# A first load in two parts, x by eight rows, and a piece of w_o cut once more, in a decode kernel of attention and a gated MLP

## The chip, the cores and the metric

The kernel runs on one core of one Trainium2 chip. The metric is the device time of one execution in microseconds. The profile comes from one execution taken by the hardware profiler; its times count from the start of the span. PE is TensorE's matmul, PEld its weight load, DVE VectorE, ACT ScalarE, POOL GpSimd, and SP SyncE, which issues most DMA transfers. One core has 16 DMA engines that all transfers share.

## What is computed

One decode step for two sequences (B = 2) of width D = 512. The normalised x feeds two branches, a windowed attention over a cache and a gated MLP; all data are float32. Cut to what matters:

```python
xn = layernorm(x)                                   # x: (2, 1, 512)
q  = xn @ wq                                        # wq: (512, 4096), 32 heads of 128
k, v = the last 4096 positions of k_cache, v_cache  # (2, 8, 4096, 128), each head used by 4 of q
s  = softmax(q @ k.T * 128 ** -0.5) @ v @ wo        # wo: (4096, 512)
z  = gelu(xn @ w_in)                                # w_in: (512, 1792)
h  = z[:896] * (w_sp * layernorm(z[896:]) + b_sp)   # w_sp and b_sp are single numbers
g  = silu(h @ w_out)                                # w_out: (896, 512)
out = x + s * g
```

The weights and the two windows together are 89.4 MB; all else is small.

## The kernel before

**Memory.** One tile `ring` (line 80) holds four slots of 32 KB in each of the 128 partitions. All large loads go through it in a fixed order: w_q in slots 0 and 1, w_in in 2, w_out in 3, then by turns the eight units of k and of v, then w_o. `enqueue` and `advance` (lines 85 to 99) issue a load on SP's queue as soon as its slots are free; a slot comes free where the code calls `advance` behind the last reader. SP issues in program order and waits at each load for the readers of the slot. Each load also waits, where eight transfers have been issued since, for the transfer that last used the same completion semaphore.

**Start.** w_q is one load of 128 rows, one row of 64 KB in each partition (`load_rows`, line 110). ScalarE issues the load of x as two rows of 512 (`xs`, lines 170 to 172), behind a tiny activation that makes its function table load early. VectorE takes mean and variance of x (`st`, `mv`, lines 210 to 213), `rsqrt` gives the scale `rs`, and a copy of it into the first element of slot 2 (line 219) makes the load of w_in wait until then. VectorE normalises (`xn`, line 233), PE turns it in four transposes into a PSUM tile, and a copy puts the two columns of each into the cleared `xnT` (lines 234 to 237), which has 32 columns per piece. The product with w_q (lines 268 to 276) needs `xnT` and all of w_q.

**Middle.** For each unit of k, VectorE turns the four quarters (`turn`), PE multiplies with q (`shares`, `add_shares`), ScalarE takes the exponentials (`probs`), and PE weighs v (`values`). The gated MLP runs ahead of the units. Small masks made on GpSimd (`same_r`, `sel`, `sel4`, `negm`) are used with the maxima of the units.

**End.** w_o is 32 blocks of rows, loaded in pieces (`load_blocks`, lines 147 to 163): one of sixteen blocks, one of eight, and a last slot with a piece of four and four single blocks. Behind the piece of sixteen SP also loads x again, as four rows for each sequence, into `x4`, which the last addition uses. The products with the first 28 blocks go to one PSUM tile `part` (lines 541 to 544), which is copied by ScalarE (`parts`) and spread by PE; the last four blocks go straight to `so`. Then come the multiplication with the gate, the addition of `x4`, and the store of the output from eight partitions (lines 557 to 560).

Lines in the profile: a helper records every operation of PE, DVE, ACT and SP, so all of these stand at line 37, and operations are told apart by their tiles.

Of the kernel before, what the change touches and what calls it, by code (L numbers as in the profile page):

```python
# [9 lines left out]
F32 = mybir.dt.float32  # L10
AF = mybir.ActivationFunctionType
ALU = mybir.AluOpType
AX = mybir.AxisListType

P = 128
HQ, DH = 32, 128
G = 4
# [4 lines left out]
def ap(t, offset, dims):  # L22

    return bass.AP(tensor=t.tensor, offset=t.offset + offset, ap=[list(t.ap[0])] + [list(d) for d in dims])
# [18 lines left out]
def kernel(  # L43
# [13 lines left out]
    nc = tc.nc  # L57
    pe, dve, act, sp = (InOrder(tc, e) for e in (nc.tensor, nc.vector, nc.scalar, nc.sync))
    B, _, D = x.shape
    _, HKV, SK, _ = k_cache.shape  # L60
    W = min(4096, max(256, SK // 4))
    REP = HQ // HKV
    F = w_in.shape[1]
    FH = F // 2
    KT = D // P
    FT = FH // P
    DC = D // G
# [5 lines left out]
    SLOT = J * DH  # L73
    BANKS = {"s": 2, "sh": 2, "acc": 2, "mo": 1, "col": 1}

    cst = ctx.enter_context(tc.tile_pool(name="cst", bufs=1))
# [3 lines left out]
    ring = cst.tile([P, 4 * SLOT], F32, tag="ring", name="ring")  # L80
# [4 lines left out]
    def enqueue(load, count=1):  # L85

        at = turns[0] % 4
        turns[0] += count
        queue.append((load, range(at, at + count)))
        advance()  # L90

    def advance(*slots):
        for n in slots:
            free[n] = True
        while queue and all(free[n] for n in queue[0][1]):
            load, at = queue.pop(0)
            for n in at:
                free[n] = False
            load(ring[:, at[0] * SLOT : (at[-1] + 1) * SLOT], at[0])

    def const(name, *shape):
        return cst.tile([P, *shape], F32, tag=name, name=name)

    def bank(name, tag):
        return ps.tile([P, 512], F32, tag=tag, name=name, bufs=BANKS[tag])
# [1 line left out]

    weight = {}

    def load_rows(name, w, k):  # L110
        def load(t, at):
            n = k * w.shape[1]
            sp.dma_start(t[:, :n], w.rearrange("(p k) f -> p (k f)", p=P))
            weight[name] = t[:, :n].rearrange("p (k f) -> p k f", k=k)

        return load

    enqueue(load_rows("q", wq, KT), 2)
    wqt = weight["q"]

    def by_group(t):
# [26 lines left out]
    blocks = []  # L148

    def load_blocks(piece):  # L150
        def load(t, at):
            t = t.rearrange("p (j d) -> p j d", d=D)
            a = 0
            for n in piece:
                j = len(blocks)
                sp.dma_start(t[:, a : a + n, :], wo_v[:, j : j + n, :])
                blocks.extend((t, a + i) for i in range(n))
                a += n
            if len(blocks) == 16:
                for b in range(B):  # L160
                    sp.dma_start(x4[16 * b : P : 32, :], x[b].rearrange("o (g c) -> (o g) c", g=G))

        return load


    ident = const("ident", P)
    make_identity(nc, ident)


    xs = cst.tile([B, D], F32, tag="xs", name="xs")  # L170
    act.activation(xs[:, 0:1], ident[:B, 0:1], AF.Ln, bias=1.0)
    act.dma_start(xs, x[:, 0, :])
    wb1 = cst.tile([1, 2], F32, tag="wb1", name="wb1")
    act.dma_start(wb1[:, 0:1], bass.AP(tensor=w_sp.tensor, offset=w_sp.offset, ap=[[1, 1], [1, 1]]))
    act.dma_start(wb1[:, 1:2], bass.AP(tensor=b_sp.tensor, offset=b_sp.offset, ap=[[1, 1], [1, 1]]))
    xnT = const("xnT", KT, 32)
    nc.gpsimd.memset(xnT, 0.0)
    ones = const("ones", P)
    nc.gpsimd.memset(ones, 1.0)
    hT = const("hT", FT, 32)  # L180
    nc.gpsimd.memset(hT, 0.0)
    x4 = const("x4", DC)
    nc.gpsimd.memset(x4, 0.0)
    add_dq = const("add_dq", NCH - 1 + P)
    nc.gpsimd.memset(add_dq, 0.0)
    sel = const("sel", 56)
# [10 lines left out]
    grpm = const("grpm", G)  # L197
    dve.tensor_reduce(grpm, ident.rearrange("p (g c) -> p g c", g=G), axis=AX.X, op=ALU.add)

    def rsqrt(dst, a, tag):  # L200
        t = cst.tile(list(a.shape), F32, tag="rt" + tag, name="rt" + tag)
        act.activation(t, a, AF.Ln)
        act.activation(dst, t, AF.Exp, scale=-0.5)
        dve.tensor_mul(t, dst, dst)
        dve.tensor_mul(t, t, a)
        dve.tensor_scalar(t, t, -0.5, 1.5, op0=ALU.mult, op1=ALU.add)
        dve.tensor_mul(dst, dst, t)


    st = cst.tile([B, nc.vector.BN_STATS_DIM], F32, tag="st", name="st")  # L210
    dve.bn_stats(st, xs)
    mv = cst.tile([B, nc.vector.BN_AGGR_DIM], F32, tag="mv", name="mv")
    dve.bn_aggr(mv, st)
    va = cst.tile([B, 1], F32, tag="va", name="va")
    dve.tensor_scalar_add(va, mv[:, 1:2], EPS)
    rs = cst.tile([B, 1], F32, tag="rs", name="rs")
    rsqrt(rs, va, "x")

    dve.tensor_copy(ring[:B, 2 * SLOT : 2 * SLOT + 1], rs)
    enqueue(load_rows("in", w_in, KT))  # L220
    enqueue(load_rows("out", w_out, FT))
    win, wout = weight["in"], weight["out"]
    for n in range(NU + 1):
# [2 lines left out]
        if n > 0:  # L226
            enqueue(load_unit(v_cache, units[n - 1], "v"))

    for piece in ((16,), (8,), (4, 1, 1, 1, 1)):
        enqueue(load_blocks(piece))  # L230

    xn = cst.tile([B, D], F32, tag="xn", name="xn")
    dve.tensor_scalar(xn, xs, mv[:, 0:1], rs, op0=ALU.subtract, op1=ALU.mult)
    pt = bank("xnT_ps", "sh")[:, : KT * B].rearrange("p (k b) -> p k b", k=KT)
    for k in range(KT):
        pe.transpose(pt[:, k, :], xn.rearrange("b (p k) -> b k p", k=KT)[:, k, :], ident[:B, :B])
    dve.tensor_copy(xnT[:, :, :B], pt)

    same = const("same", G, 32)
    nc.gpsimd.tensor_copy(same, ap(rowm, 0, [[0, G], [1, 32]]))  # L240
# [28 lines left out]
    for k in range(KT):  # L269
        for r in range(2):  # L270
            for g in range(G):
                c = (r * G + g) * 512
# [5 lines left out]
    qT = sb.tile([P, 1024], F32, tag="qT", name="qT", bufs=1)  # L278
# [3 lines left out]
    for gs in range(G):  # L282
        for b in range(B):
            dve.tensor_scalar_mul(
                ap(qm, b * 128 + gs // 2 * 32 + gs % 2 * 4, [[64, 2], [8, 4], [1, REP]]),
                ap(qT, b, [[512, 2], [32, 4], [128, REP]]), grpm[:, gs : gs + 1],
            )
    rp = bank("rp", "mo")[:, : 2 * B * 64]
    pe.matmul(rp, same, qm, start=True, stop=True)
# [23 lines left out]
    zt = const("zt", 2 * FT, 32)  # L313
    dve.transpose(zt.rearrange("p j c -> p (j c)"), ap(zs, 0, [[FQ, 2], [1, FT], [FT, 32]]))
    zT = const("zT", 2, FT, B)
    zTf = zT.rearrange("p h j b -> p (h j) b")
    dve.tensor_copy(zTf, zt[:, :, :B])
    uu = const("u", 2, FT, B)
    dve.tensor_mul(uu, zT, zT)
    dve.tensor_scalar(uu, uu, 0.044715, 1.0, op0=ALU.mult, op1=ALU.add)  # L320
# [34 lines left out]
    for j in range(FT):  # L355
        g = j % G
# [111 lines left out]
    def gather(b):  # L468

        hq = sb.tile([P, 32], F32, tag="hq", name=f"hq{b}")  # L470
        by_d = col[0][32 * b : 32 * b + 32, :].rearrange("p (j d) -> p d j", j=NCH)
        for e in range(4):
            dve.reduce_sum(hq[32 * e : 32 * e + 32, :], by_d[:, 32 * e : 32 * e + 32, :], axis=AX.X)
        t = bank(f"oT{b}", "acc")[:, :32]
        pe.matmul(t, perm, hq, start=True, stop=True)
        return t
# [56 lines left out]
    t = gather(last.b)  # L533
# [7 lines left out]
    for n in range(EARLY):  # L541
        t, a = blocks[n]
        g = n % G
# [4 lines left out]
    for n in range(EARLY, 32):  # L548
        if n == LATE:
            spread_quarters(so, parts, start=False, stop=False)  # L550
        t, a = blocks[n]
# [37 lines left out]
```

## Time and profile before

| | us |
|---|---|
| median of 3 runs | 218.07 (217.55 to 218.26) |
| span of the profiled execution | 215.6 |
| PE busy | 144.9 |
| DVE busy | 107.1 |
| ACT busy | 43.7 |
| POOL busy | 4.2 |
| share of the 16 DMA engines | 96.9% on the queue of SP |

The page gives for the profiled execution its span, 215.6 us; the device time of the runs holds some 2.5 us around such a span. A row of the chain of waits has a start, a length and what ran; a row of the timeline has a start, a length, the engine, the operation and its tiles, with the idle time before it and what ended that in brackets. A row of stretches has its bounds and its length, the busy time of five engines, the granted clock of PE, the mean busy share of the DMA engines and their GB/s; a packet's whole time counts in the stretch in which it starts, so a short stretch can show a share above 1. The queue table has packets, megabytes and the share of 16 engines' time; q1 is SP's queue, q10 that of ScalarE, q8 carries the fetches of instructions. Where a window is asked for, it starts with a row of GB/s in 40 equal slices of that window.

### The profile page before, as it was taken

The numbers are of one execution on the slowest core, as the hardware profiler recorded it, in microseconds if no ns is written. First come the engines' busy times: TensorE is split into PE (matmuls) and PEld (weight loads), VectorE is DVE, ScalarE is ACT, GpSimd is POOL, SyncE is SP. The second block draws the span as 40 slices with busy tenths as digits, with TensorE's granted clock in tenths as the row PEclk, the third lists the DMA queues.
The fourth block names the chain that finished last, engine by engine and source line by source line (L and its number), as shares of the span: only waits on it lengthen the run. The fifth ranks groups of instructions, "written<-read, shape, count | busy, mean of one in ns | idle before, by whom it ended". The sixth has DMA issues, their size and how long they took to land.

```text
span 215.6 us, 2181 instructions
## 1 busy us (share of the span) xinstructions
PE 144.9 (67%) x848; PEld 40.3 (19%) x848; DVE 107.1 (50%) x161; ACT 43.7 (20%) x108; POOL 4.2 (2%) x22
## 2 busy tenths in 40 slices
PE   0010787224595897699599499459949967987663
PEld 0010222100021222122122132112202211222311
DVE  1140025633995943953936663793585089233101
ACT  2030000331124115114303304130331231241001
POOL 6010000000000000000000000000000000000000
PEclk9999999658599699699799789859975996999998
DMA  9898999999999999999999999999999999999990
GB/s 389 390 389 389 431 423 459 435 438 421 450 395 474 395 453 419 444 432 425 439 404 450 419 444 429 432 432 419 444 413 447 425 432 444 425 435 404 410 376 33
DMA packets 3788, 89.52 MB, mean 415 GB/s; under 512 B 434, under 2 KB 450, under 8 KB 964
## 3 DMA queue, kind: packets, MB, share of 16 engines
q1 hardware_dynamic: 3772, 89.40, 96.9%
q8 instruction: 6, 0.10, 0.2%
q14 instruction: 2, 0.02, 0.0%
q10 hardware_dynamic: 8, 0.00, 0.0%
HBM read 89.40 MB, written 0.00 MB: 415 GB/s over the span
## 4 chain that ended last, share of the span: by engine, by line
DMA 41%; PE 39%; DVE 16%; ACT 2%; issue 2%; DVEq 0%
DMA ring<-in_A_wo_dram 20%; PE sh L37 11%; DMA ring<-in_A_k_cache_dram 11%; DVE kt L37 10%; DMA ring<-in_A_wq_dram 10%; PE s L37 10%; PE acc L37 7%; PE q_ps L37 4%; PE y L37 2%; PE z L37 1%; PE col L37 1%; PE mo L37 1%; DVE gate L37 1%; DVE u L37 1%; DVE qm L37 1%
## 5 line engine op out<-in xcount | busy, mean ns | idle before, releaser
L37 DVE STREAM_TRANSPOSE kt<-ring 128x2048 f32<-128x2048 f32 x32 | 72.2, 2286 | 24.9 <-DMA ring<-in_A_k_cache_dram 24.9
L37 PE MATMUL sh<-kt,qbd 128*32 128x512 f32 x256 | 43.6, 725 | 27.0 <-DVE kt L37 27.0
L37 ACT ACTIVATE shs<-sh 128x512 f32<-128x512 f32 x32 | 19.1, 597 | 99.4 <-PE sh L37 99.4
L37 PE MATMUL s<-shs,add_dq 128*128 128x512 f32 x64 | 39.0, 716 | 0.0
L37 PE MATMUL acc<-ring,pT 128*32 128x512 f32 x256 | 31.3, 614 | 0.0
L37 PEld LDWEIGHTS s<-shs,add_dq 128*128 128x128 f32 x64 | 11.0, 215 | 30.9 <-issue 26.5
L37 PEld LDWEIGHTS sh<-kt,qbd 128*32 128x32 f32 x256 | 7.0, 117 | 46.3 <-issue 38.3
L37 PE MATMUL q_ps<-ring,xnT 128*32 128x512 f32 x64 | 8.8, 713 | 7.6 <-DMA ring<-in_A_wq_dram 7.6
L37 PEld LDWEIGHTS acc<-ring,pT 128*32 128x32 f32 x256 | 7.8, 112 | 22.3 <-issue 17.6
L37 DVE TENSOR_REDUCE m<-s 128x2 f32<-128x512 f32 x8 | 5.4, 680 | 13.0 <-PE s L37 12.9
L37 PE MATMUL xnT_ps<-ident,xn 2*128 2x2 f32 x4 | 0.6, 252 | 14.5 <-DVE xn L37 14.5
L37 ACT ACTIVATE o<-acc,diag 128x128 f32<-128x128 f32 x30 | 8.6, 374 | 4.9 <-PE acc L37 4.9
L37 PE MATMUL part<-ring,oT 128*32 128x512 f32 x56 | 6.6, 597 | 3.5 <-DMA ring<-in_A_wo_dram 3.5
L37 ACT ACTIVATE p<-s,nb 128x256 f32<-128x256 f32 x16 | 7.6, 488 | 6.6 <-DVE nb L37 6.4
L37 DVE STREAM_TRANSPOSE qT<-q_ps 128x512 f32<-128x512 f32 x2 | 1.4, 717 | 14.4 <-PE q_ps L37 14.3
L37 PE MATMUL col<-o,sel 128*32 128x512 f32 x14 | 7.3, 601 | 0.0
L37 DVE TENSOR_TENSOR res<-so,gate 128x128 f32<-128x128 f32 x1 | 0.3, 292 | 11.5 <-PE so L37 11.5
L37 DVE STREAM_TRANSPOSE pT<-p 128x512 f32<-128x512 f32 x8 | 5.4, 674 | 1.2 <-ACT p L37 1.2
L37 PE MATMUL y<-ring,hT 128*32 128x512 f32 x14 | 3.3, 996 | 3.8 <-DVE hT L37 3.8
L37 ACT ACTIVATE zs<-z 128x448 f32<-128x448 f32 x1 | 0.5, 544 | 24.7 <-PE z L37 24.7
L37 ACT ACT_TABLE_LOAD x4 | 5.1, 1283 | 0.8 <-PEq L575 0.7
L37 PEld LDWEIGHTS q_ps<-ring,xnT 128*32 128x32 f32 x64 | 2.5, 130 | 13.1 <-issue 13.1
(114 smaller groups left out, 62.2 us busy)
## 6 DMA issues: line engine op xcount, KB each, us to landing
ring<-in_A_k_cache_dram SPq DMA_DIRECT2D x8, 4096.0 KB, 20.0
ring<-in_A_v_cache_dram SPq DMA_DIRECT2D x8, 4096.0 KB, 28.1
ring<-in_A_wo_dram SPq DMA_DIRECT2D x1, 4096.0 KB, 33.2
ring<-in_B_w_in_dram SPq DMA_DIRECT2D x1, 3584.0 KB, 17.1
ring<-in_A_wo_dram SPq DMA_DIRECT2D x1, 2048.0 KB
ring<-in_B_w_out_dram SPq DMA_DIRECT2D x1, 1792.0 KB, 21.0
ring<-in_A_wo_dram SPq DMA_DIRECT2D x1, 1024.0 KB
ring<-in_A_wo_dram SPq DMA_DIRECT2D x4, 256.0 KB, 17.6
```

Source lines behind the costliest of these rows:

```text
L37: return self.tc.keep_in_program_order(call(*args, **kwargs))
```

## The change

Three edits. The load of w_q is cut into two transfers, rows 0 to 15 and rows 16 to 127. x is loaded once, by ScalarE, onto partitions 0, 16, 32 and so on of a cleared tile of 128 partitions: eight rows, each of the two sequences four times. The statistics are taken on all 128 partitions; four subtractions, one on each 32 partitions, each take their own quarter of the columns, GpSimd copies the same quarters to `x4`, and one transposition on VectorE makes `xnT` in place of PE's four and a copy. The sequences then stand in columns 0 and 16 of `xnT`, so the readers of `qT` and `zt` step by 16. SP's two loads of `x4` go. The last slot of w_o holds a piece of three blocks and five single ones.

```diff
-    def load_rows(name, w, k):
+    def load_rows(name, w, k, cuts=(0, P)):
         def load(t, at):
             n = k * w.shape[1]
-            sp.dma_start(t[:, :n], w.rearrange("(p k) f -> p (k f)", p=P))
+            for a, b in zip(cuts, cuts[1:]):
+                sp.dma_start(t[a:b, :n], w.rearrange("(p k) f -> p (k f)", p=P)[a:b])
...
-    enqueue(load_rows("q", wq, KT), 2)
+    enqueue(load_rows("q", wq, KT, (0, 16, P)), 2)
...
-            if len(blocks) == 16:
-                for b in range(B):
-                    sp.dma_start(x4[16 * b : P : 32, :], x[b].rearrange("o (g c) -> (o g) c", g=G))
...
-    xs = cst.tile([B, D], F32, tag="xs", name="xs")
-    act.activation(xs[:, 0:1], ident[:B, 0:1], AF.Ln, bias=1.0)
-    act.dma_start(xs, x[:, 0, :])
+    xs = const("xs", D)
+    nc.gpsimd.memset(xs, 0.0)
+    act.activation(xs[:, 0:1], ident[:, 0:1], AF.Ln, bias=1.0)
+    act.dma_start(xs[0:P:16, :], bass.AP(tensor=x.tensor, offset=x.offset, ap=[[0, G], [D, B], [1, D]]))
...
-    for piece in ((16,), (8,), (4, 1, 1, 1, 1)):
+    for piece in ((16,), (8,), (3, 1, 1, 1, 1, 1)):
         enqueue(load_blocks(piece))
 
-    xn = cst.tile([B, D], F32, tag="xn", name="xn")
-    dve.tensor_scalar(xn, xs, mv[:, 0:1], rs, op0=ALU.subtract, op1=ALU.mult)
-    pt = bank("xnT_ps", "sh")[:, : KT * B].rearrange("p (k b) -> p k b", k=KT)
-    for k in range(KT):
-        pe.transpose(pt[:, k, :], xn.rearrange("b (p k) -> b k p", k=KT)[:, k, :], ident[:B, :B])
-    dve.tensor_copy(xnT[:, :, :B], pt)
+    xn = const("xn", DC)
+    for g in range(G):
+        r = slice(32 * g, 32 * g + 32)
+        dve.tensor_scalar(
+            xn[r, :], xs[r, g * DC : (g + 1) * DC], mv[r, 0:1], rs[r, :], op0=ALU.subtract, op1=ALU.mult
+        )
+        nc.gpsimd.tensor_copy(x4[r, :], xs[r, g * DC : (g + 1) * DC])
+    xnT = const("xnT", KT, 32)
+    dve.transpose(xnT.rearrange("p k c -> p (k c)"), ap(xn, 0, [[1, KT], [KT, 32]]))
...
-                ap(qT, b, [[512, 2], [32, 4], [128, REP]]), grpm[:, gs : gs + 1],
+                ap(qT, 16 * b, [[512, 2], [32, 4], [128, REP]]), grpm[:, gs : gs + 1],
...
-    dve.tensor_copy(zTf, zt[:, :, :B])
+    dve.tensor_copy(zTf, zt[:, :, 0 : 16 * B : 16])
```

In SP's program the first rows are these, before with a minus and after with a plus; the numbers are rows by elements of each transfer.

```order
-L584 UNCONDITIONAL_BRANCH
-L37 DMA ring<-in_A_wq_dram 128x16384
+L583 UNCONDITIONAL_BRANCH
+L37 DMA ring<-in_A_wq_dram 16x16384
+L37 DMA ring<-in_A_wq_dram 112x16384
 L37 DMA ring<-in_B_w_in_dram 128x7168
 L37 DMA ring<-in_B_w_out_dram 128x3584
```

One transfer became two, both ahead of w_in.

At the start of VectorE's program, from the statistics of x to `xnT`, before:

```order
L37 BN_STATS st<-xs 2x6
L37 BN_AGGR mv<-st 2x2
L37 TENSOR_SCALAR va<-mv 2x1
L37 TENSOR_TENSOR rtx<-rs 2x1
L37 TENSOR_TENSOR rtx<-rtx,va 2x1
L37 TENSOR_SCALAR rtx<-rtx 2x1
L37 TENSOR_TENSOR rs<-rs,rtx 2x1
L37 COPY ring<-rs 2x1
L37 TENSOR_SCALAR xn<-xs,mv,rs 2x512
L37 COPY xnT<-xnT_ps 128x4x2
```

And the same place after the change:

```order
L37 BN_STATS st<-xs 128x6
L37 BN_AGGR mv<-st 128x2
L37 TENSOR_SCALAR va<-mv 128x1
L37 TENSOR_TENSOR rtx<-rs 128x1
L37 TENSOR_TENSOR rtx<-rtx,va 128x1
L37 TENSOR_SCALAR rtx<-rtx 128x1
L37 TENSOR_TENSOR rs<-rs,rtx 128x1
L37 COPY ring<-rs 128x1
L37 TENSOR_SCALAR xn<-xs,mv,rs 32x128 x4
L37 STREAM_TRANSPOSE xnT<-xn 128x128
```

The copy that releases w_in (`ring<-rs`) keeps its place; behind it one instruction became four, and the copy from PSUM became a transposition.

The end of SP's program, from the piece of eight blocks on, with what each row waits for (DMAHW is an earlier transfer's completion); before:

```order
L37 DMA ring<-in_A_wo_dram 128x4096 [waits DMAHW3_49,DVE_49]
L37 DMA ring<-in_A_wo_dram 128x2048 [waits DMAHW4_49,PE_49]
L37 DMA ring<-in_A_wo_dram 128x512 x2
L37 DMA ring<-in_A_wo_dram 128x512 [waits DMAHW5_49]
L37 DMA ring<-in_A_wo_dram 128x512 [waits DMAHW6_49]
L37 DMA out_dram<-res 4x2x128 [waits DMAHW7_49,DVE_49]
```

After:

```order
L37 DMA ring<-in_A_wo_dram 128x4096 [waits DMAHW4_49,DVE_49]
L37 DMA ring<-in_A_wo_dram 128x1536 [waits DMAHW5_49,PE_49]
L37 DMA ring<-in_A_wo_dram 128x512 [waits PE_49]
L37 DMA ring<-in_A_wo_dram 128x512 x3
L37 DMA ring<-in_A_wo_dram 128x512 [waits DMAHW6_49]
L37 DMA out_dram<-res 4x2x128 [waits DMAHW7_49,DVE_49]
```

Five singles follow a shorter piece, and the first of them waits for PE by itself. The last single waited for the completion of the piece of sixteen blocks and now waits for that of the last load of v.

More of the change, by code (lines that the diff above doesn't have):

```diff
@@ L175 @@
     act.dma_start(wb1[:, 1:2], bass.AP(tensor=b_sp.tensor, offset=b_sp.offset, ap=[[1, 1], [1, 1]]))
-    xnT = const("xnT", KT, 32)
-    nc.gpsimd.memset(xnT, 0.0)
     ones = const("ones", P)
@@ L182 @@
     x4 = const("x4", DC)
-    nc.gpsimd.memset(x4, 0.0)
     add_dq = const("add_dq", NCH - 1 + P)
@@ L207, in rsqrt @@
         dve.tensor_mul(dst, dst, t)
-    st = cst.tile([B, nc.vector.BN_STATS_DIM], F32, tag="st", name="st")
+    st = const("st", nc.vector.BN_STATS_DIM)
     dve.bn_stats(st, xs)
-    mv = cst.tile([B, nc.vector.BN_AGGR_DIM], F32, tag="mv", name="mv")
+    mv = const("mv", nc.vector.BN_AGGR_DIM)
     dve.bn_aggr(mv, st)
-    va = cst.tile([B, 1], F32, tag="va", name="va")
+    va = const("va", 1)
     dve.tensor_scalar_add(va, mv[:, 1:2], EPS)
-    rs = cst.tile([B, 1], F32, tag="rs", name="rs")
+    rs = const("rs", 1)
     rsqrt(rs, va, "x")
-    dve.tensor_copy(ring[:B, 2 * SLOT : 2 * SLOT + 1], rs)
+    dve.tensor_copy(ring[:, 2 * SLOT : 2 * SLOT + 1], rs)
     enqueue(load_rows("in", w_in, KT))
```

## The prediction

> **What bounds the kernel now.** I read the page's DMA part first, then the busy share of the DMA engines by stretch, then the chain that ended last, then single transfers. The page's queue table, then stretches cut where the start and the end of the transfers show; their last two columns are DMA share and GB/s.
>
> ```profile
> q1 hardware_dynamic: 3772, 89.40, 96.9%
> q8 instruction: 6, 0.10, 0.2%
> q10 hardware_dynamic: 8, 0.00, 0.0%
> ...
> 1.74:2.20 0.46, 0.00 (x0) 0.00 (x0) 0.27 (x2) 0.45 (x2) 0.46 (x6) 1.00 6.64 2280
> 4.60:5.30 0.70, 0.00 (x0) 0.00 (x0) 0.00 (x0) 0.00 (x0) 0.00 (x0) 1.00 3.46 1498
> ...
> 31.00:200.00 169.00, 127.21 (x691) 34.56 (x684) 101.71 (x138) 39.97 (x102) 0.00 (x0) 0.86 1.00 431
> 200.00:209.40 9.40, 5.92 (x52) 1.63 (x49) 0.55 (x2) 0.00 (x0) 0.00 (x0) 1.00 0.98 406
> 209.40:210.00 0.60, 0.59 (x8) 0.16 (x8) 0.00 (x0) 0.00 (x0) 0.00 (x0) 1.00 0.75 277
> 210.00:211.10 1.10, 1.09 (x24) 0.41 (x16) 0.00 (x0) 0.50 (x1) 0.00 (x0) 1.00 0.47 179
> 211.10:211.60 0.50, 0.38 (x16) 0.35 (x16) 0.00 (x0) 0.10 (x1) 0.00 (x0) 1.00 0.18 66
> ```
>
> The sixteen DMA engines never rest: share 1.00 at 431 GB/s from 31 to 200 us and 0.98 to 209.4. A packet's whole time is booked where it starts, hence 6.64 in the short row: 6.64 x 0.46 = 3.05 us for the first packet of each engine, 3.46 x 0.70 = 2.42 us for the second. Both are one 64 KB row of w_q. So the first row costs 0.63 us more than the next.
>
> The end is uneven: from 210.0 to 211.1 only 0.47 of the engines still work. The reason is in two small windows, one around an instruction fetch, one that holds only a packet that followed such a fetch.
>
> ```profile
> q1 hardware_dynamic: 16, 0.52, 103.7%
> q8 instruction: 1, 0.02, 5.3%
> ...
> DMA packets 1, 0.03 MB, mean 328 GB/s; under 512 B 0, under 2 KB 0, under 8 KB 0
> ...
> q1 hardware_dynamic: 1, 0.03, 105.9%
> ```
>
> The fetch held one engine for 5.3% of 16 x 1.2 us = 1.02 us (window 39.5 to 40.7); the 32 KB packet behind one took 105.9% of 16 x 0.1 us = 1.69 us (194.9 to 195.0), where 32 KB at 431/16 GB/s takes 1.22. A fetched engine thus ends 1.02 + 0.47 = 1.5 us late, and there are six such fetches: these engines work alone at the end. Behind them stands the end of the chain, and the output's issue from the timeline.
>
> ```profile
> 201.98 9.97 DMA ring<-in_A_wo_dram
> 211.94 0.04 issue
> 211.99 0.47 PE so L37 x8
> ...
> 212.48 0.30 DVE res L37
> ...
> 212.81 0.29 DVE res L37
> ...
> 213.12 0.60 SPq L37 DMA_DIRECT2D out_dram<-res  x1
> ```
>
> So the time is: when the engines start, plus 89.4 MB at line rate, plus 1.5 us on a fetched engine, plus a tail of 215.6 - 211.94 = 3.7 us that the change leaves alone. The chain names 201.98 only because the last single block of w_o was issued then; the engines had other blocks until 209.4, so its issue is not late.
>
> **w_q as 16 and 112 rows.** What it can change is the start. The first 2.2 us, in 40 slices of 0.055 us, and the issue itself:
>
> ```profile
> GB/s 0 0 0 0 0 0 0 0 0 0 0 0 0 0 0 0 0 0 0 0 0 0 0 0 0 0 0 0 0 0 0 3575 1192 3575 1192 2383 3575 0 1192 2383
> DMA packets 16, 1.05 MB, mean 477 GB/s; under 512 B 0, under 2 KB 0, under 8 KB 0
> ...
> 0.73 0.39 SPq L37 DMA_DIRECT2D ring<-in_A_wq_dram  x1
> 13.92 0.34 SPq L37 DMA_DIRECT2D ring<-in_B_w_in_dram  x1
> 14.30 0.44 SPq L37 DMA_DIRECT2D ring<-in_B_w_out_dram  x1
> ```
>
> The sixteen first packets start between slice 32 (1.71 us) and slice 40 (2.2 us): about 0.44 us apart, 0.03 per engine. If that spread is the making of eight row entries per engine, one entry each shrinks it. The nearest row is the output: two rows on each of four engines.
>
> ```profile
> GB/s 0 0 0 0 0 0 0 0 0 0 0 0 0 0 20 61 62 21 0 0 0 0 0 0 0 0 0 0 0 0 0 0 0 0 0 0 0 0 0 0
> DMA packets 12, 0.00 MB, mean 4 GB/s; under 512 B 4, under 2 KB 12, under 8 KB 12
> ```
>
> In slices of 0.025 us from 214.0, its packets lie in four slices; its four engines begin within two, 0.05 us, at most 0.017 each. Sixteen at that pace spread over 0.25 us, 0.2 less than now; with one row still less. Its first packet comes 1.24 us after its issue began (213.12 to slice 15, 214.36), so the earliest engine has nothing to gain: w_q's waited 1.0. The gain at the last engine lies between 0.6 (spread gone, and first rows at the restart's excess of 0.47 instead of 0.63) and a loss of 0.1 (an issue of 0.44 instead of 0.34). I take **0.25**. The second issue, some 0.4 us later, is covered: the first rows run until 4.7 us. Its own completion packet per engine costs below 0.01.
>
> [...]
>
> **w_o's piece of four as three and one.** The weight loads for the pieces, from PEld's timeline:
>
> ```profile
> 206.90 0.16 PEld L37 LDWEIGHTS part<-ring,oT 128*32 128x32 f32 x8 [2.08 <-DMA ring<-in_A_wo_dram]
> 209.41 0.16 PEld L37 LDWEIGHTS part<-ring,oT 128*32 128x32 f32 x8 [1.49 <-DMA ring<-in_A_wo_dram]
> 210.70 0.16 PEld L37 LDWEIGHTS so<-ring,oT 128*32 128x32 f32 x8 [0.28 <-DMA ring<-in_A_wo_dram]
> 211.25 0.16 PEld L37 LDWEIGHTS so<-parts,rowm 128*32 128x32 f32 x8 [0.39 <-ACT parts L37]
> 211.99 0.16 PEld L37 LDWEIGHTS so<-ring,oT 128*32 128x32 f32 x8 [0.36 <-DMA ring<-in_A_wo_dram]
> ```
>
> Four blocks at once came 2.51 us after the piece ahead (206.90 to 209.41), 0.63 a block; four singles took 2.58 (to 211.99), 0.645. One more single costs **0.02 to 0.05**; I take 0.03. What it frees is PE's side: three of the four blocks are there some 0.6 us earlier, so the copy to "parts" and its spreading (211.25) move forward. But PE then waited 0.36 us for the last block anyway: off the path, worth nothing, though it gives room if the last block comes earlier. The added issue is covered: even the last single of today, issued at 201.98, is early by the seven us that the engines stay full (to 209.4).
>
> **x loaded once.** Removed are two loads of four 512 B rows on SP, four transposes of PE and a copy; added are a wider clearing, four subtractions, a turning on VectorE and four copies on GpSimd. None is on the path unless x comes too late for w_in:
>
> ```profile
> 10.19 0.68 DVE L37 BATCH_NORM_STATS2 st<-xs 2x6 f32<-2x512 f32 x1 [8.18 <-DMA xs<-in_A_x_dram]
> 13.82 0.53 DVE L37 TENSOR_SCALAR xn<-xs,mv,rs 2x512 f32<-2x512 f32 x1
> ...
> 22.67 7.52 PE L37 MATMUL q_ps<-ring,xnT 128*32 128x512 f32 x52 [7.57 <-DMA ring<-in_A_wq_dram]
> ...
> L37 DVE STREAM_TRANSPOSE qT<-q_ps 128x512 f32<-128x512 f32 x2 | 1.4, 717 | 14.4 <-PE q_ps L37 14.3
> ...
> L193 POOL MEMSET oT<- 128x1024 f32 x1 | 1.0, 952 | 0.0
> ...
> 0.73 1.28 ACT L37 ACT_TABLE_LOAD   x1 [0.73 <-PEq L575]
> ...
> 67.77 0.38 PE mo L37 x2
> ...
> DMA packets 32, 0.46 MB, mean 765 GB/s; under 512 B 16, under 2 KB 16, under 8 KB 16
> ```
>
> x's packets take turns with w_q's rows, one per 2.42 us. Today two engines carry one row and one completion each. Spread like the output, over four engines, each carries two rows: x lands one turn later, 12.6 us, and w_in, 3.73 us behind it (10.19 to 13.92), is issued at 16.3. The last row is of the window 21.6 to 22.2: sixteen completions of w_q and sixteen first packets of w_in. With 1.0 to 1.4 us from issue to first packet, w_in must be issued by about 20.2: 3.9 us of room. The normalised x follows: four subtractions of 128 columns, each at most the 0.53 us of the one of 512, and a turning of 128 columns, at most the 0.72 of one of 512. From 13.82 + 2.42 that ends by 19.1, ahead of w_q at 22.67. The clearing of x on GpSimd, half of the 0.95 us of a tile twice as wide, ends near 1.4; the ScalarE instruction that now waits for it, with x's load queued behind it, stands behind a table load until 2.0. Were it late, x would lose one more turn of 2.42, within the room. GpSimd's four copies wait for x, and behind them the small masks of the maxima, first used at 67.77. Term: **0**, between -0.07 and +0.1 on four engines.
>
> **Sum**, against the profiled execution's 215.6 us: -0.25 + 0.03 + 0.01 = -0.2, so 215.4. The median of the runs is 2.5 us above that span, which nothing here touches: 218.07 - 0.2 = **217.9 us**. A measurement of this kernel tells apart about 0.3%, 0.65 us; the forecast is below that.
>
> **Rivals.**
> 1. *The start does not move.* The spread belongs to the handing over to sixteen engines, not to rows; for it speaks that w_q's earliest engines (three in one slice) are as close as the output's. Then only the costs stay: 218.1. Chance 0.28. [...]
> 2. *The first rows also lose their excess.* If the 0.63 us were the making of 128 entries, 0.44 + 0.63 = 1.07 goes: 217.1. Against it: the packet behind a fetch has 0.47 of excess with no issue near it. Chance 0.13.
> 3. *w_in comes late and the engines run dry* at 22 us. It decides when x lands after 16.5 us. On two engines as now, four rows each, x lands at 10.19 + 3 x 2.42 = 17.4, w_in is issued at 21.2, its packets start at 22.2 to 22.6 where rows end at 21.6 to 22.2: about 0.8 us dry, 218.7. On one engine it would be 27.1 and 10 us. For it: x now has more rows than engines. Against: the output of the same form, 4 x 2 rows, shows 12 packets, eight rows and four completions. Chance 0.06.
> 4. *Two fetches meet on one engine*: +1.5 us, 219.4. Here 0.47 x 16 = 7.5 engines work on after 210.0, which fits six fetches on six engines. Chance 0.03.
>
> The forecast has 0.50. **Faster** by over 0.3% (below 217.4) is most of rival 2 and a little of the forecast: 0.15. **Slower** (above 218.7) is half of rival 3, rival 4 and the runs' own scatter (217.55 to 218.26): 0.08. **Same**: 0.77. The range, 217.1 to 218.6, takes in rivals 1 and 2 and leaves the rest out.
>
> **What will show it.** In the changed profile: sixteen first packets within 0.25 us or less (forecast), still 0.44 (rival 1); their mean near 3.0 us, or near 2.42 (rival 2); x's statistics start near 12.6 us and w_in's issue near 16.3, with DMA share 1 at 22 us, or a hole there (rival 3); "parts" copied some 0.6 us earlier relative to the last block, with PE still waiting for that block. Wrong would be a last landing that moves by more than 0.6 us without a hole at 22 us, or a start that shrinks while the end stays.

## The result: 21 us slower

The changed kernel takes 239.19 us (median of 6 runs, 238.20 to 239.54) against 217.81 for the kernel before (6 runs): a ratio of 1.0985, with a 95% interval of 1.0965 to 1.1005. The forecast was 217.9 us, with a range of 217.1 to 218.6. The profiled execution has a span of 237.0 us, 21.4 more than before.

The kernel before and the changed one: from each page the GB/s of its 40 slices, from the changed page also the busy share of the DMA engines in the slices and the queue table.

```profile
GB/s 389 390 389 389 431 423 459 435 438 421 450 395 474 395 453 419 444 432 425 439 404 450 419 444 429 432 432 419 444 413 447 425 432 444 425 435 404 410 376 33
...
DMA  9879979999999999999999999999999999999980
GB/s 177 177 178 300 232 177 235 387 416 466 426 412 422 437 443 443 437 418 437 415 420 436 431 443 437 431 437 429 426 420 426 440 437 431 431 443 415 400 333 15
...
q1 hardware_dynamic: 3916, 89.40, 96.6%
```

The first row is the kernel before, the others the changed one. The share of the DMA engines is still 96.6%, and its slices read 7 to 9 from the start. The GB/s tell the story: in the first seven slices (41 us) the engines are busy and move 177 to 300 GB/s, where the kernel before moved 389 from its first slice. So the time in which a packet crawls counts as busy too. The load of w_q and the product behind it in the chain of waits, before and after, and two stretches of the changed kernel:

```profile
0.73 21.80 DMA ring<-in_A_wq_dram
22.67 8.85 PE q_ps L37 x64
...
1.20 42.84 DMA ring<-in_A_wq_dram
44.03 0.14 issue
44.17 8.42 PE q_ps L37 x64
```

```profile
43.10:220.00 176.90, 133.70 (x740) 35.66 (x740) 101.61 (x136) 39.96 (x102) 0.00 (x0) 0.87 1.00 430
2.30:43.10 40.80, 0.00 (x0) 0.00 (x0) 4.57 (x21) 1.69 (x3) 3.76 (x15) 1.00 0.82 201
```

The product with w_q starts at 44.17 us and not at 22.67: 21.5 us, the whole difference. From 43.1 on all runs as before, 430 GB/s at share 1.00. The second transfer of w_q takes 42.84 us from its issue; together the two carry the 8.4 MB that one transfer brought in 21.8.

How long each row of 64 KB took shows in short stretches, each of which holds the starts of one row on all sixteen engines; share times length is the mean time of a row.

```profile
1.70:2.30 0.60, 0.00 (x0) 0.00 (x0) 0.54 (x2) 0.52 (x2) 0.60 (x6) 1.00 14.32 1748
9.50:11.40 1.90, 0.00 (x0) 0.00 (x0) 0.00 (x0) 0.00 (x0) 0.00 (x0) 1.00 2.79 552
15.20:16.30 1.10, 0.00 (x0) 0.00 (x0) 0.00 (x0) 0.00 (x0) 0.00 (x0) 1.00 4.29 961
19.90:20.90 1.00, 0.00 (x0) 0.00 (x0) 0.00 (x0) 0.00 (x0) 0.00 (x0) 1.00 3.31 1057
23.20:25.60 2.40, 0.00 (x0) 0.00 (x0) 0.98 (x3) 0.00 (x0) 0.90 (x4) 1.00 1.59 437
26.90:29.10 2.20, 0.00 (x0) 0.00 (x0) 1.50 (x8) 0.49 (x2) 0.00 (x0) 1.00 2.06 477
31.10:33.70 2.60, 0.00 (x0) 0.00 (x0) 0.14 (x1) 0.00 (x0) 0.04 (x1) 1.00 1.78 403
35.70:38.30 2.60, 0.00 (x0) 0.00 (x0) 0.00 (x0) 0.00 (x0) 0.00 (x0) 1.00 1.73 403
```

The first row, the transfer of 16, took 14.32 x 0.60 = 8.6 us; the seven of the transfer of 112 took 5.3, 4.7, 3.3, 3.8, 4.5, 4.6 and 4.5 us. Before, a row took 2.42 us (the first 3.05). So the loss is not an idle engine or a late issue: every row of w_q runs slower, at 0.28 to 0.73 of the rate that 2.42 us stands for.

### The profile page after: what moved, and what is told of

Its sections match the earlier page's. It is cut to its first block, busy times and chain, and to the rows that moved or that the text cites. A ratio compares the mean times of both kernels' runs of the same rounds, so it can differ in the third digit from the quotient of the medians.

```text
span 237.0 us, 2179 instructions
## 1 busy us (share of the span) xinstructions
PE 143.6 (61%) x844; PEld 39.2 (17%) x844; DVE 108.4 (46%) x164; ACT 43.7 (18%) x108; POOL 5.5 (2%) x25
## 3 DMA queue, kind: packets, MB, share of 16 engines
q1 hardware_dynamic: 3916, 89.40, 96.6%
## 4 chain that ended last, share of the span: by engine, by line
DMA 56%; PE 26%; DVE 15%; issue 1%; SPq 1%; DVEq 0%
DMA ring<-in_A_k_cache_dram 30%; DMA ring<-in_A_wq_dram 18%; DVE kt L37 12%; PE sh L37 8%; DMA ring<-in_A_wo_dram 8%; PE s L37 8%; PE acc L37 5%; PE q_ps L37 4%; PE mo L37 1%; SPq L37 1%; PE col L37 1%; DVE m L37 1%; DVE pT L37 1%; DVE mx L37 0%; DVE nb L37 0%
## 5 line engine op out<-in xcount | busy, mean ns | idle before, releaser
L37 PE MATMUL sh<-kt,qbd 128*32 128x512 f32 x256 | 43.0, 715 | 27.8 <-DVE kt L37 27.8
L37 PE MATMUL acc<-ring,pT 128*32 128x512 f32 x256 | 32.1, 629 | 0.0
L37 DVE BATCH_NORM_STATS2 st<-xs 128x6 f32<-128x512 f32 x1 | 0.7, 695 | 22.2 <-DMA xs<-in_A_x_dram 22.2
L37 PE MATMUL part<-ring,oT 128*32 128x512 f32 x56 | 7.2, 597 | 3.1 <-DMA ring<-in_A_wo_dram 3.1
```

The costliest lines, as they stand in the source:

```text
L37: return self.tc.keep_in_program_order(call(*args, **kwargs))
```

## The experiments

Four theories stood. **P**: the rows collide where they are written in SBUF, since a transfer of 16 or of 112 partitions is dealt to the engines in another way than one of 128. **H**: they collide where they are read in HBM. **T**: two open transfers slow each other, or the odd number of rows per engine does. **X**: x's eight rows hold back w_q.

**Which edit.** First the changed kernel with w_q whole again, then the kernel before with nothing but the cut.

```diff
-    enqueue(load_rows("q", wq, KT, (0, 16, P)), 2)
+    enqueue(load_rows("q", wq, KT), 2)
```

> The changed kernel with w_q in one transfer again; x by eight rows and w_o's cut stay. Theory P (w_q's rows collide where they are written, because a transfer of 16 or 112 partitions is dealt to the engines in another way than one of 128): the loss goes entirely, w_q ends near 22 us, and what is left are x and w_o: 217.9 us, 217.4 to 218.4; x's statistics start at 12.6 us and w_in is issued at 16.3. Theory X (x on four engines holds back w_q and w_in): still near 239, w_q's rows still at 4 to 8 us each.

Measured: 218.02 us against 217.56, ratio 1.0013 (0.9998 to 1.0027).

```diff
-    enqueue(load_rows("q", wq, KT), 2)
+    enqueue(load_rows("q", wq, KT, (0, 16, P)), 2)
```

Here and in the next run `load_rows` is that of the change.

> The kernel before with w_q as 16 and 112 rows and nothing else. Theory P: all of the loss, 238 to 240 us, first rows 8 to 9 us each, w_q's end near 43 us. Theory X: 217.9.

Measured: 239.0 us in one run, against 217.56 for the kernel before; the product with w_q starts at 44.40. So the cut is the whole loss, and X falls. The start of the product in the run with the cut alone; behind it, from the run with w_q whole, the stretch of one row, when x arrived, and when w_in was issued:

```profile
44.40 8.36 PE L37 MATMUL q_ps<-ring,xnT 128*32 128x512 f32 x64 [17.85 <-DMA ring<-in_A_wq_dram]
...
16.70:17.60 0.90, 0.00 (x0) 0.00 (x0) 0.83 (x5) 0.00 (x0) 0.00 (x0) 1.00 2.71 1165
...
13.11 0.69 DVE L37 BATCH_NORM_STATS2 st<-xs 128x6 f32<-128x512 f32 x1 [10.78 <-DMA xs<-in_A_x_dram]
...
16.94 0.33 SPq L37 DMA_DIRECT2D ring<-in_B_w_in_dram  x1
```

2.71 x 0.90 = 2.44 us a row again; x is 2.9 us later than before and w_in is issued at 16.94, well ahead of the 20.2 that the prediction had as its limit.

**Any cut, or this one.** w_q in two halves of 64 rows, and in two transfers along the columns that each cover all 128 partitions.

```diff
-    enqueue(load_rows("q", wq, KT), 2)
+    enqueue(load_rows("q", wq, KT, (0, 64, P)), 2)
```

> The kernel before with w_q as 64 and 64 rows, four rows to an engine. Theory P: 64 partitions reach half of the places of writing, so each half runs at no more than half rate: w_q ends at 38 to 42 us, 234 to 238 us in all. Theory N (the odd number of 7 rows per engine, or one row per engine, is what is slow): w_q ends near 22 us, 218.

Measured: 239.05 us, in one run. A row's stretch:

```profile
17.00:17.80 0.80, 0.00 (x0) 0.00 (x0) 0.00 (x0) 0.00 (x0) 0.00 (x0) 1.00 6.40 1311
```

6.40 x 0.80 = 5.12 us for this row; the engines moved 178 GB/s from 2.3 to 22.2 us and 210 from there to 44. Four and four rows an engine are slow too, so it is not the odd number. The 234 to 238 expected was a little low: a row takes more than twice 2.42, eight times some 0.28 us.

```diff
-    def load_rows(name, w, k):
+    def load_rows(name, w, k, cuts=(0, 1)):
...
-            sp.dma_start(t[:, :n], w.rearrange("(p k) f -> p (k f)", p=P))
+            for a, b in zip(cuts, cuts[1:]):
+                c = slice(n * a // cuts[-1], n * b // cuts[-1])
+                sp.dma_start(t[:, c], w.rearrange("(p k) f -> p (k f)", p=P)[:, c])
...
-    enqueue(load_rows("q", wq, KT), 2)
+    enqueue(load_rows("q", wq, KT, (0, 1, 4)), 2)
```

> The kernel before with w_q also in two transfers, but cut along the columns: a quarter of each of the 128 rows, then three quarters. Theory P: every transfer covers all 128 partitions, full rate, w_q ends near 22 us, 217.5 to 218.5. Theory T (two open transfers into one tile slow each other): 230 or more.

Measured: 217.48 against 217.56 us, ratio 0.9991 (0.9978 to 1.0004).

```profile
2.30:21.50 19.20, 4.25 (x20) 1.15 (x20) 3.36 (x17) 1.69 (x3) 2.44 (x9) 0.95 0.99 425
```

These two transfers, each over all partitions, cost nothing: 425 GB/s while w_q comes in. T falls.

**Read side or write side.** w_q in eight transfers of 16 rows. Each takes either 16 neighbouring rows of w_q or every eighth one, and puts them in 16 neighbouring partitions or in every eighth one: four kernels, which differ in one line. This is the first:

```diff
-    def load_rows(name, w, k):
+    def load_rows(name, w, k, parts=1):
...
-            sp.dma_start(t[:, :n], w.rearrange("(p k) f -> p (k f)", p=P))
+            rows = w.rearrange("(p k) f -> p (k f)", p=P)
+            for j in range(parts):
+                m = P // parts
+                near, far = slice(m * j, m * j + m), slice(j, P, parts)
+                sp.dma_start(t[near, :n], rows[near])
...
-    enqueue(load_rows("q", wq, KT), 2)
+    enqueue(load_rows("q", wq, KT, 8), 2)
```

The others have `t[far, :n], rows[far]`, then `t[far, :n], rows[near]`, then `t[near, :n], rows[far]` in the last line of the loop. The last two put rows of w_q into other partitions than those of x, so only the times of the load are read from them.

> The kernel before with w_q in eight transfers of 16 rows, each of 16 neighbouring rows of w_q to 16 neighbouring partitions. The first row of the changed kernel took 8 to 9 us; here all eight do. Theory P (the place of writing): 64 to 74 us for w_q, 258 to 270 us in all. Theory H (rows read close together in HBM): the same.

> Eight transfers of 16 rows, each of every eighth row of w_q to every eighth partition, so the result is that of the kernel before. [...] Theory H: rows are 512 KB apart in HBM; if closeness was the trouble, full rate, 218.

> Read as in the run with neighbouring rows, written as in the run with every eighth partition; w_q's rows so stand in other partitions than x's, and q is not the reference's. [...] Theory H: the time of the run near to near, 258 to 270.

> Read every eighth row, written to 16 neighbouring partitions; q is not the reference's. Theory P: the time of the run near to near, 258 to 270. Theory H: the time of the run far to far.

| read from w_q | written to partitions | one run, us | a row, us |
|---|---|---|---|
| neighbouring rows | neighbouring | 272.86 | 9.35 |
| every eighth | every eighth | 240.18 | 5.13 |
| neighbouring rows | every eighth | 239.27 | 5.13 |
| every eighth | neighbouring | 273.99 | 9.36 |

The kernel before took 217.38 us beside them. The last column comes from these stretches, in the table's order, one of each kernel:

```profile
37.60:39.80 2.20, 0.00 (x0) 0.00 (x0) 0.00 (x0) 0.00 (x0) 0.00 (x0) 1.00 4.25 477
```

```profile
16.70:18.20 1.50, 0.00 (x0) 0.00 (x0) 1.13 (x6) 0.20 (x1) 0.00 (x0) 1.00 3.42 699
```

```profile
17.00:18.00 1.00, 0.00 (x0) 0.00 (x0) 0.83 (x6) 0.00 (x0) 0.00 (x0) 1.00 5.13 1049
```

```profile
37.70:39.20 1.50, 0.00 (x0) 0.00 (x0) 0.00 (x0) 0.00 (x0) 0.00 (x0) 1.00 6.24 699
```

The place of writing decides; how the rows are read made no difference here (9.35 and 9.36 us to neighbouring partitions, 5.13 both times to every eighth). H falls. The two runs to neighbouring partitions lie above the 258 to 270 us expected, because a row took 9.35 us and not the 8 to 9 of the changed kernel's first row. The time of a row goes with the partitions that a transfer writes: 9.35 us for 16 neighbours, 3.9 times the 2.42 of the load over all 128; 5.13 for every eighth partition, 2.1 times, and much the same for 64 neighbours (5.12). The number of partitions alone doesn't give it: 16 spread over all took as long as 64 in a row. What in the writing makes these times, no trace shows.

**How 112 rows are dealt.** These reach nearly all partitions and were slow all the same. If each engine gets seven neighbouring rows, then step j of all engines is every seventh partition from 16 + j on. That can be written out:

```diff
-    def load_rows(name, w, k):
+    def load_rows(name, w, k, dealt=False):
...
-            sp.dma_start(t[:, :n], w.rearrange("(p k) f -> p (k f)", p=P))
+            rows = w.rearrange("(p k) f -> p (k f)", p=P)
+            sets = [slice(0, 16)] + [slice(16 + j, P, 7) for j in range(7)] if dealt else [slice(0, P)]
+            for s in sets:
+                sp.dma_start(t[s, :n], rows[s])
...
-    enqueue(load_rows("q", wq, KT), 2)
+    enqueue(load_rows("q", wq, KT, True), 2)
```

> The kernel before with w_q as 16 rows and then seven transfers of 16 rows, every seventh partition from 16 + j on. If the 112 rows of the changed kernel are dealt to the engines as seven neighbouring rows each (theory C), these seven transfers are the same rows on the same engines at the same steps: the row times of the changed kernel come back, about 8.5, 5.3, 4.7, 3.2, 3.8, 4.5, 4.6, 4.4 us, w_q's end at 41 to 44 us, 236 to 241 in all. Theory I (dealt one row to each engine in turn, so 16 neighbours at every step): then these transfers, which spread each step over all partitions, are faster than the changed kernel's, 7 steps of 2.4 to 3 us, w_q's end near 30 us, 225 to 229.

Measured: 239.22 us, in one run. The stretches of its eight rows:

```profile
1.70:2.60 0.90, 0.00 (x0) 0.00 (x0) 0.30 (x2) 0.51 (x2) 0.90 (x6) 1.00 9.38 1165
9.10:11.20 2.10, 0.00 (x0) 0.00 (x0) 0.00 (x0) 0.00 (x0) 0.00 (x0) 1.00 2.62 499
15.20:16.40 1.20, 0.00 (x0) 0.00 (x0) 0.00 (x0) 0.00 (x0) 0.00 (x0) 1.00 4.00 877
20.00:21.20 1.20, 0.00 (x0) 0.00 (x0) 0.65 (x5) 0.37 (x2) 0.00 (x0) 1.00 2.55 874
23.20:25.70 2.50, 0.00 (x0) 0.00 (x0) 0.55 (x3) 0.00 (x0) 0.40 (x3) 1.00 1.50 419
26.80:29.30 2.50, 0.00 (x0) 0.00 (x0) 0.00 (x0) 0.00 (x0) 0.00 (x0) 1.00 1.78 419
30.80:33.80 3.00, 0.00 (x0) 0.00 (x0) 0.00 (x0) 0.00 (x0) 0.00 (x0) 1.00 1.55 350
35.60:38.40 2.80, 0.00 (x0) 0.00 (x0) 0.00 (x0) 0.00 (x0) 0.00 (x0) 1.00 1.61 375
```

8.4, 5.5, 4.8, 3.1, 3.8, 4.5, 4.7 and 4.5 us: the changed kernel's eight rows, each within 0.3 us, down to the fast fourth one. So 112 rows behave as seven neighbouring rows to an engine. The trace doesn't name the engine of a packet, so the dealing is inferred from this pattern. For 128 rows it can't be eight neighbours in order, since partitions 0, 8, 16 and so on at a time is the run with every eighth partition: 5.13 us a row, where the whole load took 2.42.

**The small terms.** Three more kernels: all three edits with w_q cut along its columns, then x's edit alone, then w_o's alone. The first is the changed kernel with the columns' `load_rows` from above.

> The changed kernel with w_q cut along its columns, a quarter and three quarters, in place of 16 and 112 rows: all three edits without the collision. Theory P: 217.3 to 218.2, no difference that the runs can tell. x's packets then take turns with rows of 16 KB, so x lands earlier than in the kernel before (10.2 us).

Measured: 217.96 against 217.52 us, ratio 1.0024 (1.0010 to 1.0037). x's statistics start at 8.30 us there. The main lines of x's edit, as in the change:

```diff
+    xs = const("xs", D)
+    nc.gpsimd.memset(xs, 0.0)
+    act.dma_start(xs[0:P:16, :], bass.AP(tensor=x.tensor, offset=x.offset, ap=[[0, G], [D, B], [1, D]]))
...
```

> The kernel before with x by eight rows alone. The prediction's term was 0 with x a turn of 2.42 us later; the run with w_q whole and both small edits had x at 13.1 us and a ratio of 1.0013. If x carries that: 1.001 to 1.002; if w_o does: 0.9995 to 1.0005.

Measured: ratio 1.0022 (1.0006 to 1.0038).

```diff
-    for piece in ((16,), (8,), (4, 1, 1, 1, 1)):
+    for piece in ((16,), (8,), (3, 1, 1, 1, 1, 1)):
```

> The kernel before with w_o's last slot as three blocks and five single ones alone. The prediction's term was +0.03 us, a ratio of 1.0001; if the cut itself costs what the run with both small edits showed, 1.001 to 1.002.

Measured: ratio 1.0014 (1.0005 to 1.0023). By its ratio each small edit alone costs 0.3 to 0.5 us, and neither gains. Both together cost 1.0013 with w_q whole and 1.0024 with w_q by columns; the second interval reaches 1.0037, so whether they add is not settled. The spans of the runs tell a part of where the tenths sit. With x's edit alone the device time is longer than the span by a median of 2.12 us, in the kernel before by 1.81, while the span grows from 215.7 to 215.9: 0.3 of x's 0.5 us lie outside the span, where the profile shows nothing. With w_o's edit alone the difference stays at 1.79, and the span grows to 216.0. What makes these tenths stays open: the profile of w_o's edit alone has x's statistics at 10.50 us and not at 10.19, in a stretch that its code doesn't touch.

```profile
10.50 0.68 DVE L37 BATCH_NORM_STATS2 st<-xs 2x6 f32<-2x512 f32 x1 [8.49 <-DMA xs<-in_A_x_dram]
```

No version was faster than the kernel before by more than its interval.

## Why the prediction was wrong, step by step

**The step that failed** is the first sentence on w_q's cut: "What it can change is the start." It took the rate of the steady state as a property of the sixteen engines, whatever set of partitions a transfer covers. Every large transfer in the trace of before covers all 128 partitions, so no row there could show the rate of 16 or 112, and the term should have been given as unknown, with an end on the slow side. It was bounded by 0.6 us of gain and 0.1 of loss, from rows about starting; it measured 21.5 us of loss. The rows are 8.6 and 3.3 to 5.3 us long instead of 2.42. In place of a rate of the engines, the runs show a rate that depends on the partitions to which the rows at work are written: 9.35 us a row to neighbours and 5.13 to every eighth, with the same rows read.

**The rivals.** None of the four named it. The slower one, that engines run dry before w_in, did not happen: x's statistics start at 24.55 us and w_in is issued at 28.39, but w_q's slow rows kept the engines busy until 43 us.

```profile
24.55 0.69 DVE L37 BATCH_NORM_STATS2 st<-xs 128x6 f32<-128x512 f32 x1 [22.22 <-DMA xs<-in_A_x_dram]
...
28.39 0.35 SPq L37 DMA_DIRECT2D ring<-in_B_w_in_dram  x1
```

**The start itself** did not shrink as forecast. In the first 2.3 us of the changed kernel, in slices of 0.0575 us, the sixteen first packets lie between slice 31 and slice 40: 0.46 to 0.58 us apart, where the forecast said 0.25 or less and the kernel before had 0.44. Fifteen of them lie within five slices, but the term was about the last engine, and that one gained nothing by having one row instead of eight. As far as the start goes, rival 1 came out. In the run with columns the ratio is 0.9991: a gain of 0.25 us is neither shown nor excluded there.

```profile
GB/s 0 0 0 0 0 0 0 0 0 0 0 0 0 0 0 0 0 0 0 0 0 0 0 0 0 0 0 0 0 0 2280 5699 4559 0 4559 0 0 0 0 1140
DMA packets 16, 1.05 MB, mean 456 GB/s; under 512 B 0, under 2 KB 0, under 8 KB 0
```

**x** was right in mechanism: with w_q whole it is one turn later (13.11 us, forecast 12.6) and w_in is issued at 16.94 (16.3), with nothing waiting for it (DMA share 0.99 from 22.2 us on). Its four subtractions and the turning end at 18.65 us, ahead of w_q at 22.88. The term of 0 was 0.5 us too small by its ratio, 0.3 of it outside the span.

**w_o** was read wrongly in what it frees. `part` takes the first 28 blocks. With pieces of sixteen, eight and three, the 28th block is the first single one, so the copy to `parts` still waits for a block that comes as late as before. In the changed kernel PE gets the three blocks at 230.14 us and the 28th at 230.75, and the spreading of `parts` starts 0.71 us ahead of the last block's products (232.54 to 233.25); before it was 0.74 (211.25 to 211.99). The forecast had it move forward by some 0.6 us. The cost was mis-sized as well: 0.03 us forecast, 0.3 measured by the ratio, at the edge of what these runs tell.

```profile
230.14 0.15 PEld L37 LDWEIGHTS part<-ring,oT 128*32 128x32 f32 x6 [0.87 <-DMA ring<-in_A_wo_dram]
230.75 0.14 PEld L37 LDWEIGHTS part<-ring,oT 128*32 128x32 f32 x2 [0.46 <-DMA ring<-in_A_wo_dram]
...
232.54 0.16 PEld L37 LDWEIGHTS so<-parts,rowm 128*32 128x32 f32 x8 [0.41 <-ACT parts L37]
...
233.25 0.16 PEld L37 LDWEIGHTS so<-ring,oT 128*32 128x32 f32 x8 [0.34 <-DMA ring<-in_A_wo_dram]
```

**The tail** was right: after the last landing the changed kernel takes 3.8 us to the end (233.21 to 237.0, before 3.7), and PE still waits for the last block.

**The base** was looser than the forecast's gain. The 2.5 us between span and device time, which nothing was to touch, lie between 1.74 and 2.95 us in the 29 runs of the kernel before that stand beside the last experiments, with a median of 1.81; x's edit moved them. And rival 2's sum is 218.07 - 1.07 + 0.04 = 217.0, not 217.1, just outside the range that was to take it in. Neither bears on the 21 us.

## What to carry to other kernels

In these runs only transfers over all 128 partitions kept the full rate: 2.42 us a row with w_q whole, 425 GB/s with the columns. In every stretch measured here, rows of w_q in a transfer to fewer partitions took 3.1 to 9.4 us in the mean of the sixteen engines. Whether some smaller set of partitions would be fast, no run shows. To split a large load like this one, cut it along its columns (ratio 0.9991 here) and not along its partitions (21 us or more in every run here). And when the share of busy DMA engines is high, read the GB/s beside it: here a share of 0.82 went with 201 GB/s. A price that no row of the old trace can show needs a slow end in the range.

## What the runs showed that was not expected

The seven rows of the transfer of 112 differ among themselves: 3.3 to 5.3 us in the mean of sixteen engines, though each step is spread over every seventh partition, if each engine has seven neighbouring rows. The run dealt that way by hand had the same pattern, 3.1 to 5.5. Nor are the engines of one step slowed alike: in the fourth row, 3.3 us in the mean, a packet that began at 20.78 took 28.93 x 16 x 0.01 = 4.6 us (the row's bounds are rounded):

```profile
20.77:20.79 0.01, 0.00 (x0) 0.00 (x0) 0.00 (x0) 0.00 (x0) 0.00 (x0) 1.00 28.93 6554
```

Why is open, and no run here tells it. The seven rows together took 30.7 us instead of 16.9, seven times 2.42. Sixteen rows to neighbouring partitions took 9.35 us, 112 bytes per ns for the sixteen engines together, a little more than four times the 27 that one engine reaches at full rate (64 KB in 2.42 us).
